# Banded attention and a PReLU feed-forward block in fp32: eight single PSUM banks in place of two double ones, x of a single tile taken bank by bank, and another table for the opening

## The chip, the cores and the metric

The kernel runs on one core of a Trainium2 chip. The metric is the time of one execution on the device in microseconds (us), the median of three executions. TensorE (PE) multiplies and writes to PSUM, which has eight banks of 128 x 512 fp32 numbers. VectorE (DVE), ScalarE (ACT) and GpSimd (POOL) work on SBUF, the first two on PSUM as well, and SyncE (SP) issues most of the DMAs. Each engine takes its instructions in the order in which the program lists them, so one that waits holds up all behind it on its engine.

## The reference

```python
def _attn_ref(q, k, v) -> np.ndarray:        # 8 batches, 8 heads, 576 positions, 64 wide
    B, H, S, D = q.shape
    window = 64
    scale = 1.0 / np.sqrt(D)
    scores = scale * np.matmul(q, k.transpose(0, 1, 3, 2))
    pos = np.arange(S)
    rel = pos[:, None] - pos[None, :]
    mask = (rel >= 0) & (rel < window)
    scores = np.where(mask, scores, -1000000000.0)
    scores = scores - np.max(scores, axis=-1, keepdims=True)
    attn = np.exp(scores)
    attn = attn / (np.sum(attn, axis=-1, keepdims=True) + 1e-09)
    return np.matmul(attn, v).astype(np.float32)

def _moe_ref(x, w_in, w_out, alpha) -> np.ndarray:   # x 4608 x 512, w_in 512 x 2048, w_out 2048 x 512
    h = x @ w_in
    g = np.maximum(h, 0.0) + alpha * np.minimum(h, 0.0)
    return (g @ w_out).astype(np.float32)
```

The output of the attention, with the heads side by side, is x of the second function.

## The kernel before

**Tiles and stages.** The 4608 rows are 36 tiles of 128. Four tiles make a block n of 512 rows, so there are nine blocks. The first stage does the attention of a tile t and the first product of each block; the second stage (from about 500 us) does the second product with seven products of halves in place of eight (`second(n)`). Every fp32 product is made of three passes over a high and a low part: for the first product xh with wh, xl with wh, and xh with wl.

**Attention of a tile** runs over the engines in this order. The names are those of the planner and of the texts: `s` the scores (PE, `score`, L447), `le` the mask and the row's maximum of one head (DVE, `take_least`, L456, eight for a tile), `ex` the exponential (ACT, L463, eight), `rc` the reciprocal of the sums (DVE, L467 and L468), `sc` the scaling (POOL, L472, two halves u of a tile), `tu` the turning by PE (L487, one for each half), `td` the copy of what was turned out of PSUM (ACT, L491, one for each half), `av` the product with v (PE, L503), `xh` the copy of the high part of x (ACT, L575) and `xl` the low part (DVE, L577). Tiles 0 to 7 go through alone (`attend_one`), with one pair of banks for all of it: banks 2 and 3 for even tiles, 4 and 5 for odd ones (`S_BANK`). Half u is turned into bank u of the pair. The tiles after that go two at a time (`attend_two`).

**Weights.** w_in is loaded in 16 chunks f, as 64-bit words that hold doubles. `chunk` makes floats of one: `rd` (ACT, L352), `rb` (DVE, L356, or ACT, L359), `sh` (DVE, L367), `sg` (DVE, L369) and `jn` (POOL, L371); `split` then makes its high part `wi.f.h` (ACT or POOL, L325) and its low part `wi.f.l` (POOL, L322). `REBIASED` lists the chunks whose `rb` goes to DVE.

**Cells.** `cell(n, f)` is the product of block n with chunk f, `h.n.f` (L644), into bank 0 or 1 by turns; ACT and DVE then take it out of the bank (`sl` L650, `la` L651). Of block 0 the first three cells are done as halves: `h.0.f.0` with tiles 0 and 1, `h.0.f.1` with tiles 2 and 3.

**The small table.** `signs` is four DVE instructions on 128 x 16 numbers in SBUF (L312 to L315). `ident` is a constant matrix; PE multiplies it with itself (`warm`, L307) wherever the plan finds nothing else for PE before `h.0.1.0`.

**Order.** `Program.order` plays the work through with a duration for each operation and writes each engine's order out. `SINGLE` gives the begin of each single tile, `HALVES` that of the half cells; `key=` and `earliest=` set what comes first. The tile framework then puts a wait in front of an instruction for each buffer that it shares with earlier ones. Banks 2 and 3 are one PSUM buffer of 1024 columns (`twins[0]`), and banks 4 and 5 another (`twins[1]`); the others have a buffer each. In the built program a matmul into one bank of a twin waits for a reader of the other bank, and a reader of one bank for the matmuls into the other that stand ahead of it.

**Second stage.** A block n has seven sums, in the order 1, 2, 6, 7, 5, 3, 4, in seven of the eight banks; the next block begins at the bank that follows. `O.u.i` (L748) is the product i of step u, with u = 4n to 4n + 3. At the end of a block, `u1` (ACT, L765) and `d11`, `u2`, `u3`, `u4`, `d22`, `d12`, `d21` (DVE, L756) add the sums up, each reading one bank, and four DMAs store the results (L762).

Of the kernel before, what the change touches and what calls it, by code (L numbers as in the profile page):

```python
# [9 lines left out]
F32 = mybir.dt.float32  # L10
# [14 lines left out]
CELL = 3.25  # L25
UNIT = 9.55
STEP = 1.362
SINGLE = (3.0, 3.0, 11.0, 15.0, 21.0, 32.0, 35.0, 41.0)
HALVES = (14.0, 19.0)
EARLY_HALVES = 3  # L30
PACE = 3.6
FIRST_TURN = 60.0
REBIASED = (0, 1, 2, 3, 4, 5, 6, 7, 8, 9, 10, 11, 12, 13, 14, 15)
PE_TURNED = (9, 17, 25, 33)
CONVERT_AT = {1: 0, 3: 1, 5: 2, 7: 3}
LAGS = {"PE": 0.25, "DVE": 0.14, "ACT": 0.13, "POOL": 0.10, "SP": 0.0}
# [157 lines left out]
def banded_attention_then_prelu_ffn(  # L194
# [11 lines left out]
    nc = tc.nc  # L206
    P = 128
# [20 lines left out]
    psum = ctx.enter_context(tc.tile_pool(name="psum", bufs=1, space=PSUM))  # L228
# [4 lines left out]
    xs = [[const.tile([P, NP, BT * P], F32R, name=f"x{x}_0") for x in "hl"]]  # L233
# [28 lines left out]
    staged = [stage[:, i] for i in range(2)]  # L262
    raws.append(stage.rearrange("p x t -> p (x t)").bitcast(I32))

    banks = [psum.tile([P, 512], F32, name=f"bank_{i}") for i in range(2)]
    twins = [psum.tile([P, 1024], F32, name=f"bank_{2 + 2 * i}") for i in range(2)]
    banks += [twin[:, x * 512:(x + 1) * 512] for twin in twins for x in range(2)]
    banks += [psum.tile([P, 512], F32, name=f"bank_{i}") for i in (6, 7)]
    H_BANK, S_BANK, V_BANK = (0, 1), ((2, 3), (4, 5)), (6, 7)

    hidden = [[far.tile([P, 4, 2, HW], F32, name=f"g_{n}_{d}") for d in range(DUOS)] for n in range(NB)]
# [2 lines left out]
    def halves_of(*bs):  # L274
        return [f"bank.{b}.{i}" for b in bs for i in range(2)]

    p = Program()

    def add(name, engine, busy, emit, *args, **kw):
        p.add(name, {engine: (busy, emit)}, *args, **kw)  # L280
# [54 lines left out]
    def chunk(name, c, f, second, start=0.0):  # L335
# [17 lines left out]
        aside, k_aside = banks[V_BANK[c % 2]], halves_of(V_BANK[c % 2])  # L353
        by_vector = not second and f in REBIASED
        if by_vector:
# [80 lines left out]
    def bank_of(i):  # L436
        return banks[i].rearrange("p (e k) -> p e k", e=NP)
# [123 lines left out]
    def x_keys(part, slot, tiles=range(BT)):  # L561
        return [f"{part}.{slot}.{i}" for i in tiles]

    def x_parts(ts, by=V_BANK):
        n, i = divmod(ts[0], BT)
        here = slice(i * P, (i + len(ts)) * P)
        if len(ts) == 1:
            pieces = [(range(2), [part.rearrange("p (a x) t -> p x a t", x=2)[:, :, :, here] for part in xs[n % 2]],
                       twins[ts[0] % 2].rearrange("p (x i a q) -> p x i a q", x=2, i=2, a=2)[:, :, 0], halves_of(*by))]
        else:  # L570
            pieces = [([x], [part.rearrange("p (a x) (i q) -> p x i a q", x=2, q=P)[:, x, i:i + 2] for part in xs[n % 2]],
                       bank_of(V_BANK[x]).rearrange("p (i a) q -> p i a q", i=2), halves_of(V_BANK[x])) for x in range(2)]
        for x, to, from_, k in pieces:
            his, los = ([key for a in range(2) for y in x for key in x_keys(part, 4 * (n % 2) + 2 * a + y, range(i, i + len(ts)))] for part in ("xh", "xl"))
            p.add(f"xh.{ts[0]}.{x[0]}", {"ACT": (0.48, lambda to=to, from_=from_: nc.scalar.copy(to[0], from_)),  # L575
                                         "DVE": (0.6, lambda to=to, from_=from_: nc.vector.tensor_copy(to[0], from_))}, k, his)
            add(f"xl.{ts[0]}.{x[0]}", "DVE", 0.61, lambda to=to, from_=from_: nc.vector.tensor_tensor(  # L577
                out=to[1], in0=from_, in1=to[0].bitcast(F32), op=ALU.subtract), [*k, *his], los)

    def attend_one(t, begin, pace):  # L580
# [10 lines left out]
    def values_of(ts, key):  # L591
        def emit():
            for i, t in enumerate(ts):
                value(t, i)

        add(f"av.{ts[0]}", "PE", 2.0, emit, [*(k for t in ts for k in ring_keys("v", t)), *(k for t in ts for k in pt_keys(t))], halves_of(*V_BANK), key=key)
        x_parts(ts)
# [25 lines left out]
    def begin_of(n):  # L623
        return BEGIN + n * CELL * NF
# [155 lines left out]
    add("masks", "POOL", 3.2, guard_and_masks, (), ["masks", "sums"])  # L780
    for t, begin in enumerate(SINGLE):
        attend_one(t, begin, 5.0)
    for f in range(NF):
        convert_in(f)
    pair = lambda j: [t for t in (2 * j, 2 * j + 1) if t < NT]
    attend_two(pair(len(SINGLE) // 2), FIRST_TURN, [])
    for n in range(NB):
        for j, f in ((2 * n + 3, 4), (2 * n + 4, 12)):
            if j > len(SINGLE) // 2 and pair(j - 1):
                attend_two(pair(j), begin_of(n) + (f - 0.5) * CELL, pair(j - 1))  # L790
# [3 lines left out]
        if n == 0:  # L794
            for f in range(EARLY_HALVES):
                cell(n, f, HALVES[0] + f * PACE, 0)
            whole = NF - EARLY_HALVES
            for f in range(max(EARLY_HALVES, whole)):
                if f < EARLY_HALVES:
                    cell(n, f, HALVES[1] + f * PACE, 1)  # L800
                if f < whole:
                    cell(n, EARLY_HALVES + f, HALVES[1] + (f + 0.5) * PACE)
        if n in CONVERT_AT:
# [56 lines left out]
```

## Time and profile before

| | us |
|---|---|
| median of three runs | 857.07 |
| lowest and highest | 854.37, 858.63 |
| the profiled execution: time | 860.36 |
| the profiled execution: span on the core | 858.6 |
| PE busy (share of the span) | 847.6 (99%) |
| DVE busy | 696.8 (81%) |
| ACT busy | 438.2 (51%) |
| POOL busy | 201.9 (24%) |

The span runs from the first to the last event on the core; the execution's own time is 1.8 us longer. PE is busy nearly throughout, so the time is PE's work, what PE waits, what it loses to a lower clock or spends on `warm`, and what comes behind its last matmul.

### The profile page before, as it was taken

The page shows a single profiled execution, that of the slowest core. Times are in us where ns is not written, and L with a number is a line of the kernel's source. Part 1 is how long each engine was busy: PE and PEld are TensorE (multiplying, and loading weights), DVE is VectorE, ACT ScalarE, POOL GpSimd, SP SyncE. Part 2 cuts the span into 40 slices and gives each one's busy share as a digit, 9 for nine tenths or more (in the row PEclk, how much of TensorE's full clock was granted, in tenths as well). Part 3 has the DMA queues.
Part 4 walks back from the last instruction along what each step waited for, and adds up shares of the span by engine and source line. Part 5 has one row for each costly group of instructions (what it writes and reads, how often), then busy time and mean ns, then how long its engine had stood idle before and what let it go on. Part 6 is the DMA issues. An engine that isn't in the chain of part 4 may idle for free.

```text
span 858.6 us, 21067 instructions
## 1 busy us (share of the span) xinstructions
PE 847.6 (99%) x7850; PEld 769.2 (90%) x7850; DVE 696.8 (81%) x1777; ACT 438.2 (51%) x1110; POOL 201.9 (24%) x190
## 2 busy tenths in 40 slices
PE   8899999999999999999999999999999999999997
PEld 8788888888888888888888899999999999999997
DVE  5797898998989989899876367978888786979783
ACT  6787765466454664457534244444444444444440
POOL 5788391116411363113720000000000000000000
PEclk9899999999999999999999999999999999999999
DMA  8787655565556666566447995544444343535201
GB/s 254 237 261 240 216 166 167 166 199 175 193 173 186 230 203 234 170 222 234 167 173 257 291 341 177 160 134 125 124 144 146 116 147 111 159 107 165 72 30 50
DMA packets 121287, 152.91 MB, mean 178 GB/s; under 512 B 10592, under 2 KB 92512, under 8 KB 121184
## 3 DMA queue, kind: packets, MB, share of 16 engines
q1 hardware_dynamic: 120896, 151.30, 55.2%
q8 instruction: 62, 1.02, 0.5%
q14 instruction: 41, 0.34, 0.1%
q10 hardware_dynamic: 288, 0.26, 0.1%
HBM read 95.95 MB, written 55.57 MB: 176 GB/s over the span
## 4 chain that ended last, share of the span: by engine, by line
PE 97%; ACT 1%; DVE 1%; issue 0%; POOL 0%; DVEq 0%; POOLq 0%
PE bank L644 46%; PE bank L748 41%; PE bank L503 4%; PE bank L447 4%; PE bank L487 1%; ACT w L463 1%; PE bank L307 1%; ACT pt L491 0%; DVE cell L756 0%; DVE xl L577 0%; DVE alphas L312 0%; ACT ulps L352 0%; DVE val L369 0%; POOL w L472 0%; DVE w L456 0%
## 5 line engine op out<-in xcount | busy, mean ns | idle before, releaser
L720 ACT CAST yh<-g 128x512 fp32r<-128x512 f32 x216 | 132.7, 621 | 146.2 <-PE bank L748 94.7
L650 ACT ACTIVATE cell<-bank,alphas 128x512 f32<-128x512 f32 (+1 forms) x147 | 99.8, 679 | 175.7 <-PE bank L644 168.9
L721 DVE TENSOR_TENSOR yl<-g,yh 128x512 fp32r<-128x512 f32 x216 | 147.7, 687 | 28.8 <-ACT yh L720 27.2
L748 PE MATMUL bank<-wh,yh 128*128 128x256 f32 x1008 | 159.0, 280 | 0.8 <-DVE cell L756 0.8
L748 PE MATMUL bank<-wh,yl 128*128 128x256 f32 x1008 | 158.9, 280 | 0.0
L748 PE MATMUL bank<-wl,yh 128*128 128x256 f32 x1008 | 158.9, 280 | 0.0
L644 PE MATMUL bank<-xh,wh 128*128 128x512 f32 (+1 forms) x588 | 158.6, 392 | 0.0
L644 PE MATMUL bank<-xl,wh 128*128 128x512 f32 (+1 forms) x588 | 155.3, 386 | 0.0
L644 PE MATMUL bank<-xh,wl 128*128 128x512 f32 (+1 forms) x588 | 154.6, 385 | 0.0
L651 DVE SCALAR_TENSOR_TENSOR cell<-bank,alphas,cell 128x512 f32<-128x512 f32 (+1 forms) x147 | 108.4, 739 | 55.5 <-ACT cell L650 51.0
L748 PEld LDWEIGHTS bank<-wh,yh 128*128 128x128 f32 x1008 | 136.5, 189 | 1.1 <-ACT yh L720 1.0
L748 PEld LDWEIGHTS bank<-wh,yl 128*128 128x128 f32 x1008 | 135.7, 189 | 0.0
L748 PEld LDWEIGHTS bank<-wl,yh 128*128 128x128 f32 x1008 | 135.6, 189 | 0.0
L644 PEld LDWEIGHTS bank<-xl,wh 128*128 128x128 f32 x588 | 109.6, 189 | 22.6
L644 PEld LDWEIGHTS bank<-xh,wl 128*128 128x128 f32 x588 | 109.3, 188 | 22.1
L644 PEld LDWEIGHTS bank<-xh,wh 128*128 128x128 f32 x588 | 107.6, 189 | 22.8 <-issue 0.5
L463 ACT ACTIVATE w<-w,nm 128x128 f32<-128x128 f32 x288 | 111.6, 391 | 23.2 <-DVE nm L456 23.2
L472 POOL TENSOR_TENSOR w<-w,rc 128x512 f32<-128x512 f32 x72 | 74.3, 1052 | 136.3 <-DVE rc L468 100.0
L480 DVE STREAM_TRANSPOSE pt<-w 32x256 f32<-32x256 f32 x192 | 83.7, 436 | 9.6 <-POOL w L472 6.1
L715 DVE TENSOR_TENSOR g<-g,g 128x512 f32<-128x512 f32 x108 | 74.2, 687 | 1.8
L456 DVE CUSTOM_DVE_ANT_0 w<-bank,masks 128x128 f32<-128x128 f32 x288 | 63.0, 286 | 8.7 <-PE bank L447 8.7
L482 DVE STREAM_TRANSPOSE pt<-w 32x128 f32<-32x128 f32 x192 | 58.1, 303 | 3.9
(62 smaller groups left out, 701.7 us busy)
## 6 DMA issues: line engine op xcount, KB each, us to landing
g<-g SPq DMA_DIRECT2D x144, 256.0 KB, 3.3
g<-cell SPq DMA_DIRECT2D x141, 256.0 KB, 3.1
out<-cell SPq DMA_DIRECT2D x36, 256.0 KB, 2.5
q<-qT SPq DMA_DIRECT2D x35, 256.0 KB, 5.0
raw<-w_out SPq DMA_DIRECT2D x16, 512.0 KB, 5.8
v<-vN SPq DMA_DIRECT2D x18, 384.0 KB, 5.1
k<-kT SPq DMA_DIRECT2D x17, 384.0 KB, 4.5
raw<-w_in SPq DMA_DIRECT2D x11, 512.0 KB, 5.4
```

The source lines that it names most:

```text
L456: nc.vector.tensor_tensor_reduce(out=of_head(weights[t % 2], g), in0=bank_of(S_BANK[t % 2][x])[:, e].rearrange("p (b k) -> p b k", b=2), i ...
L463: nc.scalar.activation(w, w, AF.Exp, scale=-1.0, bias=least[t % 2][:, g:g + 1], accum_out=sums[:, t % 2, g, 0:1])
L472: nc.gpsimd.tensor_tensor(out=w, in0=w, in1=rc.unsqueeze(1).unsqueeze(3).broadcast_to(list(w.shape)), op=ALU.mult)
L480: nc.vector.transpose(to, w[:, x, j])
L482: nc.vector.transpose(to[:, :, j ^ 1], w[:, x, j, :, j ^ 1])
L644: nc.tensor.matmul(h, w[KEPT + f][:, a * P:(a + 1) * P], v[:, a, half], start=k == a == 0, stop=k == 2 and a == NP - 1, skip_group_check=True)
L650: add(f"sl.{name}", "ACT", 0.13 + 0.46 * part, lambda: nc.scalar.activation(g, h, AF.Copy, scale=slope[:, f:f + 1]), ["signs", *k_h], k_g)
L651: add(f"la.{name}", "DVE", 0.12 + 0.61 * part, lambda: nc.vector.scalar_tensor_tensor(out=g, in0=h, scalar=sign[:, f:f + 1], in1=g, op0=AL ...
L715: add(name, "DVE", 0.61, lambda: nc.vector.tensor_tensor(out=to(), in0=a(), in1=b(), op=op), reads, writes)
L720: add(f"ys.{u}.{i}.h", "ACT", 0.54, lambda: nc.scalar.copy(y_of(y_hi, x, hi), value()), [*ks, "late"], his)
L721: add(f"ys.{u}.{i}.l", "DVE", 0.61, lambda: nc.vector.tensor_tensor(out=y_of(y_lo, x, lo), in0=value(), in1=y_of(y_hi, x, hi).bitcast(F32) ...
L748: nc.tensor.matmul(banks[bank][:, h * EH:(h + 1) * EH], part[:, j * HW + h * P:j * HW + (h + 1) * P], w[k][:, j * EH:(j + 1) * EH], start= ...
```

## The change

Each PSUM bank becomes a buffer of its own. For a single tile, x is copied (`xh`) and subtracted (`xl`) in two instructions of 256 columns, one for each bank, where one instruction of 512 columns took both. The chunks whose `rb` goes to DVE are six and no longer sixteen; the other ten go to ACT. Four numbers of the table of turns are others, and the planner's durations for the x of a single tile are those of the smaller pieces.

```diff
-SINGLE = (3.0, 3.0, 11.0, 15.0, 21.0, 32.0, 35.0, 41.0)
-HALVES = (14.0, 19.0)
+SINGLE = (3.0, 3.0, 11.0, 13.0, 23.0, 32.0, 37.0, 41.0)
+HALVES = (12.0, 19.0)
...
-REBIASED = (0, 1, 2, 3, 4, 5, 6, 7, 8, 9, 10, 11, 12, 13, 14, 15)
+REBIASED = (1, 4, 5, 7, 8, 9)
...
-    banks = [psum.tile([P, 512], F32, name=f"bank_{i}") for i in range(2)]
-    twins = [psum.tile([P, 1024], F32, name=f"bank_{2 + 2 * i}") for i in range(2)]
-    banks += [twin[:, x * 512:(x + 1) * 512] for twin in twins for x in range(2)]
-    banks += [psum.tile([P, 512], F32, name=f"bank_{i}") for i in (6, 7)]
+    banks = [psum.tile([P, 512], F32, name=f"bank_{i}") for i in range(8)]
...
-        here = slice(i * P, (i + len(ts)) * P)
-        if len(ts) == 1:
-            pieces = [(range(2), [part.rearrange("p (a x) t -> p x a t", x=2)[:, :, :, here] for part in xs[n % 2]],
-                       twins[ts[0] % 2].rearrange("p (x i a q) -> p x i a q", x=2, i=2, a=2)[:, :, 0], halves_of(*by))]
-        else:
-            pieces = [([x], [part.rearrange("p (a x) (i q) -> p x i a q", x=2, q=P)[:, x, i:i + 2] for part in xs[n % 2]],
-                       bank_of(V_BANK[x]).rearrange("p (i a) q -> p i a q", i=2), halves_of(V_BANK[x])) for x in range(2)]
+        copy, other, pass_ = (0.48, 0.6, 0.61) if len(ts) == 2 else (0.36, 0.34, 0.35)
+        pieces = [([x], [part.rearrange("p (a x) (i q) -> p x i a q", x=2, q=P)[:, x, i:i + len(ts)] for part in xs[n % 2]],
+                   bank_of(by[x]).rearrange("p (i a) q -> p i a q", i=2)[:, :len(ts)], halves_of(by[x])) for x in range(2)]
```

The order of the instructions differs in the opening alone (to `h.0.15` on PE); the first instructions to differ stand behind the exponentials of tile 1. Behind the opening the order is as before, and the bank buffers and the waits differ. Where rows of the two programs are set side by side, the lines of the changed kernel have smaller numbers (L367 of before is L364).

The first place is DVE between the second reciprocal of tile 1 and the first `le` of tile 2. `bank_6` and `bank_7` are where `sh` puts its result, `alphas` is the table of `signs`, `bank_2` (with `bank_3`) and `bank_4` (with `bank_5`) hold tiles 0 and 1. Before:

```order
L367 TENSOR_SCALAR bank_7_166<-bank_7_166 128x512
L577 TENSOR_TENSOR xl_0_120<-bank_2_163,xh_0_119 128x2x2x128
L369 SCALAR_TENSOR_TENSOR val_156<-raw_1_155,bank_7_166 128x512
L356 TENSOR_SCALAR bank_6_165<-stage_160 128x512
L312 TENSOR_SCALAR alphas_130<-alphas_130 128x16
L313 TENSOR_SCALAR alphas_130<-alphas_130 128x16
L314 TENSOR_TENSOR alphas_130<-alphas_130 128x16
L315 TENSOR_SCALAR alphas_130<-alphas_130 128x16
L577 TENSOR_TENSOR xl_0_120<-bank_4_164,xh_0_119 128x2x2x128
L367 TENSOR_SCALAR bank_6_165<-bank_6_165 128x512
L369 SCALAR_TENSOR_TENSOR val_156<-stage_160,bank_6_165 128x512
L456 ISA w_0_146,nm_0_150<-bank_2_163,masks_140 128x2x64
```

And now, in the same place (`xl` is L570, `signs` L309 to L312, `sh` L364, `sg` L366, `le` L453):

```order
L364 TENSOR_SCALAR bank_7_168<-bank_7_168 128x512
L366 SCALAR_TENSOR_TENSOR val_156<-raw_1_155,bank_7_168 128x512
L570 TENSOR_TENSOR xl_0_120<-bank_2_163,xh_0_119 128x2x128
L309 TENSOR_SCALAR alphas_130<-alphas_130 128x16
L310 TENSOR_SCALAR alphas_130<-alphas_130 128x16
L311 TENSOR_TENSOR alphas_130<-alphas_130 128x16
L312 TENSOR_SCALAR alphas_130<-alphas_130 128x16
L570 TENSOR_TENSOR xl_0_120<-bank_3_164,xh_0_119 128x2x128
L364 TENSOR_SCALAR bank_6_167<-val_156 128x512
L570 TENSOR_TENSOR xl_0_120<-bank_4_165,xh_0_119 128x2x128
L570 TENSOR_TENSOR xl_0_120<-bank_5_166,xh_0_119 128x2x128
L366 SCALAR_TENSOR_TENSOR val_156<-stage_160,bank_6_167 128x512
```

The low part of tile 0 stood whole ahead of `signs`; now its second half, out of bank 3, stands behind them, and the scores of tile 2, which go into banks 2 and 3, wait for both halves. `rb` of chunk 2 (L356) has gone to ACT.

The second place is POOL in the same stretch. `val` with `ulps` is `jn`, `wh_12` and `wl_12` are the parts of chunk 0, `wl_13` the low part of chunk 1. Before:

```order
L371 TENSOR_TENSOR val_156<-val_156,ulps_0_157 128x512
L325 CAST wh_12_75<-val_156 128x512
L322 TENSOR_TENSOR wl_12_103<-val_156,wh_12_75 128x512
L371 TENSOR_TENSOR val_156<-val_156,ulps_1_158 128x512
L322 TENSOR_TENSOR wl_13_104<-val_156,wh_13_76 128x512
```

And now:

```order
L368 TENSOR_TENSOR val_156<-val_156,ulps_0_157 128x512
L322 CAST wh_12_75<-val_156 128x512
L368 TENSOR_TENSOR val_156<-val_156,ulps_1_158 128x512
L319 TENSOR_TENSOR wl_12_103<-val_156,wh_12_75 128x512
L319 TENSOR_TENSOR wl_13_104<-val_156,wh_13_76 128x512
```

`jn` of chunk 1 now comes ahead of the low part of chunk 0; `wl_13` waits for `wh_13`, which ACT makes out of that `jn`.

The third place is the end of DVE's list, the adding up of the last block, `d11`, `u2`, `u3`, `u4`, `d22`, `d12`, `d21`. Before:

```order
L756 TENSOR_TENSOR cell_0_125<-bank_1_162,r_0_122 128x512
L756 TENSOR_TENSOR r_1_123<-bank_2_163,r_0_122 128x512
L756 TENSOR_TENSOR r_2_124<-bank_2_163,r_1_123 128x512
L756 TENSOR_TENSOR r_0_122<-bank_4_164,r_1_123 128x512
L756 TENSOR_TENSOR cell_3_128<-bank_4_164,r_2_124 128x512
L756 TENSOR_TENSOR cell_1_126<-bank_4_164,r_0_122 128x512
L756 TENSOR_TENSOR cell_2_127<-bank_6_165,r_2_124 128x512
```

And now:

```order
L749 TENSOR_TENSOR cell_0_125<-bank_1_162,r_0_122 128x512
L749 TENSOR_TENSOR r_1_123<-bank_2_163,r_0_122 128x512
L749 TENSOR_TENSOR r_2_124<-bank_3_164,r_1_123 128x512
L749 TENSOR_TENSOR r_0_122<-bank_4_165,r_1_123 128x512
L749 TENSOR_TENSOR cell_3_128<-bank_4_165,r_2_124 128x512
L749 TENSOR_TENSOR cell_1_126<-bank_5_166,r_0_122 128x512
L749 TENSOR_TENSOR cell_2_127<-bank_6_167,r_2_124 128x512
```

Nothing moved; the names of the buffers did. In the built program `u4` (the fourth row) waited for the matmuls of product 3, the last into the twin of banks 4 and 5; now it waits for those of product 5, the last into bank 4.

## Rows read from the trace of the kernel before

**Rows 1.** The profile's page: ACT's busy tenths in 40 slices; the last-ending chain by engine.
```profile
ACT  6787765466454664457534244444444444444440
...
PE 97%; ACT 1%; DVE 1%; issue 0%; POOL 0%; DVEq 0%; POOLq 0%
```

**Rows 2.** Chain that ended last, in order: start us, us, what.
```profile
23.30 6.27 ACT w L463 x32
...
31.82 1.99 PE bank L503 x48
...
37.84 1.06 PE bank L503 x48
```

**Rows 3.** Windows of 1 us: us, each engine's busy time, PE's granted clock, DMA.
```profile
30.00:31.00 1.00, 0.79 (x4) 0.56 (x4) 0.96 (x5) 0.63 (x2) 0.45 (x1) 0.69 0.14 50
...
37.00:38.00 1.00, 1.00 (x14) 0.86 (x17) 0.00 (x0) 1.00 (x3) 0.59 (x1) 0.90 0.05 17
```

**Rows 4.** Timeline of DVE: start us, us, instruction, idle before and releaser.
```profile
14.22 0.67 DVE L367 TENSOR_SCALAR bank<-bank 128x512 int32<-128x512 int32 x1
...
19.36 1.28 DVE L312 TENSOR_SCALAR alphas<-alphas 128x16 f32<-128x16 f32 x1
20.67 0.17 DVE L313 TENSOR_SCALAR alphas<-alphas 128x16 f32<-128x16 f32 x1
...
22.97 0.28 DVE L456 CUSTOM_DVE_ANT_0 w<-bank,masks 128x128 f32<-128x128 f32 x1
```

**Rows 5.** Timeline of POOL.
```profile
17.39 0.61 POOL L325 CAST wh<-val 128x512 fp32r<-128x512 f32 x1
18.09 1.29 POOL L322 TENSOR_TENSOR wl<-val,wh 128x512 fp32r<-128x512 f32 x1
19.33 1.27 POOL L371 TENSOR_TENSOR val<-val,ulps 128x512 int32<-128x512 int32 x1
21.33 1.27 POOL L322 TENSOR_TENSOR wl<-val,wh 128x512 fp32r<-128x512 f32 x1 [0.73 <-ACT wh L325]
```

**Rows 6.** Timeline at 85 us: a POOL and a DVE instruction.
```profile
84.80 1.30 POOL L322 TENSOR_TENSOR wl<-val,wh 128x512 fp32r<-128x512 f32 x1
...
85.29 1.09 DVE L361 TENSOR_SCALAR val<-val,alphas 128x512 int32<-128x512 int32 x1
```

**Rows 7.** Timeline of PE behind tile 1 and at the turning of tile 2.
```profile
19.92 1.83 PE L307 MATMUL bank<-ident 128*128 128x128 f32 x14
21.67 1.10 PE L447 MATMUL bank<-k,q 64*64 64x128 f32 x32
...
30.21 0.94 PE L487 MATMUL bank<-ident,w 128*128 128x128 f32 x4 [0.77 <-ACT pt L491]
```

**Rows 8.** Groups by line and form: costs of 256 columns (xcount, busy us, mean ns).
```profile
L651 DVE SCALAR_TENSOR_TENSOR cell<-bank,alphas,cell 128x256 f32<-128x256 f32 x6 | 2.8, 472 | 2.5 <-ACT cell L650 2.5
```

**Rows 9.** Timeline of ACT at the end of tile 3's exponentials.
```profile
29.10 0.39 ACT L463 ACTIVATE w<-w,nm 128x128 f32<-128x128 f32 x1
...
29.48 0.58 ACT L491 COPY pt<-bank 128x512 f32<-128x512 f32 x1
29.96 0.67 ACT L352 ACTIVATE ulps<-raw 128x512 int32<-128x512 uint32 x1
```

**Rows 10.** Timeline of DVE and PE in the second stage, at the third block.
```profile
584.47 0.68 DVE L756 TENSOR_TENSOR cell<-bank,r 128x512 f32<-128x512 f32 x1
...
585.29 0.71 PE L748 MATMUL bank<-wh,yh 128*128 128x256 f32 x4 [0.81 <-DVE cell L756]
```

**Rows 11.** Timeline of the end: DVE's last rows, PE's last, SP's last.
```profile
852.69 0.69 DVE L756 TENSOR_TENSOR r<-bank,r 128x512 f32<-128x512 f32 x1 [1.41 <-PE bank L748]
...
853.30 1.88 DVE L756 TENSOR_TENSOR cell<-bank,r 128x512 f32<-128x512 f32 x3
...
853.43 0.63 PE L748 MATMUL bank<-wh,yl 128*128 128x256 f32 x4
854.00 1.57 SPq L762 DMA_DIRECT2D out<-cell  x3
```

More of the change, by code (lines that the diff above doesn't have):

```diff
@@ L565, in x_parts @@
         n, i = divmod(ts[0], BT)
-        here = slice(i * P, (i + len(ts)) * P)
-        if len(ts) == 1:
-            pieces = [(range(2), [part.rearrange("p (a x) t -> p x a t", x=2)[:, :, :, here] for part in xs[n % 2]],
-                       twins[ts[0] % 2].rearrange("p (x i a q) -> p x i a q", x=2, i=2, a=2)[:, :, 0], halves_of(*by))]
-        else:
-            pieces = [([x], [part.rearrange("p (a x) (i q) -> p x i a q", x=2, q=P)[:, x, i:i + 2] for part in xs[n % 2]],
-                       bank_of(V_BANK[x]).rearrange("p (i a) q -> p i a q", i=2), halves_of(V_BANK[x])) for x in range(2)]
+        copy, other, pass_ = (0.48, 0.6, 0.61) if len(ts) == 2 else (0.36, 0.34, 0.35)
+        pieces = [([x], [part.rearrange("p (a x) (i q) -> p x i a q", x=2, q=P)[:, x, i:i + len(ts)] for part in xs[n % 2]],
+                   bank_of(by[x]).rearrange("p (i a) q -> p i a q", i=2)[:, :len(ts)], halves_of(by[x])) for x in range(2)]
         for x, to, from_, k in pieces:
             his, los = ([key for a in range(2) for y in x for key in x_keys(part, 4 * (n % 2) + 2 * a + y, range(i, i + len(ts)))] for part in ("xh", "xl"))
-            p.add(f"xh.{ts[0]}.{x[0]}", {"ACT": (0.48, lambda to=to, from_=from_: nc.scalar.copy(to[0], from_)),
-                                         "DVE": (0.6, lambda to=to, from_=from_: nc.vector.tensor_copy(to[0], from_))}, k, his)
-            add(f"xl.{ts[0]}.{x[0]}", "DVE", 0.61, lambda to=to, from_=from_: nc.vector.tensor_tensor(
+            p.add(f"xh.{ts[0]}.{x[0]}", {"ACT": (copy, lambda to=to, from_=from_: nc.scalar.copy(to[0], from_)),
+                                         "DVE": (other, lambda to=to, from_=from_: nc.vector.tensor_copy(to[0], from_))}, k, his)
+            add(f"xl.{ts[0]}.{x[0]}", "DVE", pass_, lambda to=to, from_=from_: nc.vector.tensor_tensor(
                 out=to[1], in0=from_, in1=to[0].bitcast(F32), op=ALU.subtract), [*k, *his], los)
```

## The prediction

> **What bounds the kernel now.** I read the profile from the whole to the stretch. The page first: the chain that ended last is PE for 97% of the span [rows 1], so an edit elsewhere counts only where PE waits for it. Then the chain in order of time: from 31.82 us, where `av` of tile 2 begins, it is PE work without a break to the end of the first stage, and in the second stage PE waits once. So the time is settled in three places: by when `av` of tile 2 can begin, by that one wait, and by what comes behind PE's last matmul.
>
> Up to 31.82 us the chain runs through other engines. PE has done tile 1 by 19.92 us, passes 1.83 us with `warm`, and starts the scores of tile 2 at 21.67 [rows 7]. DVE begins `le` of tile 2 at 22.97 [rows 4]. ACT then works 6.27 us at the exponentials of tiles 2 and 3 [rows 2], the last from 29.10 [rows 9]; only then come the copies `td` and `av`. PE's clock is the second thing to see: the granted clock falls within 30 to 31 us and is back within 37 to 38 [rows 3]; between lies half clock, 1.2 GHz in place of 2.4, behind a stretch in which PE mostly waited. `av` took 1.99 us there and 1.06 later [rows 2].
>
> The sum is made against the profiled execution, 860.36 us, which is 1.8 us above its span and 3.3 above the median of the three runs, 857.07. I carry the difference over to the median.
>
> **Step 1, the start of tile 2 (a wait is added).** The scores of tile 2 go into banks 2 and 3, so they wait for `xl` of tile 0 out of both. That was one instruction ahead of `signs`; now its second half stands behind `signs`. What `signs` cost is in the rows: its first instruction, on 16 columns, took 1.28 us, where the next took 0.17 [rows 4]. It began at 19.36 and ended at 20.64; POOL's `jn` ran from 19.33 to 20.60 [rows 5]. At 85 us the same: a DVE instruction from SBUF to SBUF, begun at 85.29, ended 0.28 behind the end of POOL's `wl` at 86.10 [rows 6]. So such a DVE instruction waits until POOL's is done. The other three of `signs` ran fast because POOL then stood idle 0.73 us, until 21.33, for `wh` from ACT [rows 5].
>
> When does this come now? Up to the exponentials of tile 1 nothing moved. `rb` of chunk 0 is behind them on ACT, 0.67 us by the row of another ACT instruction of that size [rows 9], so DVE begins `sh` at about 14.5 where it was 14.22 [rows 4]. Then come `sh`, `rb`, `sg`, `sh`, `sg`, five of about 0.65 us: 17.7. The first half of `xl` brings it to 18.0, and there `signs` begin. POOL can start `jn` of chunk 0 when the first `sg` is done, three instructions in, at 16.5. Its next five, by [rows 5], are 1.27, 0.61, 1.27, 1.29 and 1.27: 5.7 us, to 22.2. The idle time is gone, since `jn` of chunk 1 now comes 1.29 us earlier in POOL's list, and ACT has made `wh_13` (ready about 20.8) before POOL asks for it at 20.9. So the four instructions of `signs` meet a POOL that is never idle from 16.5 to 22.2.
>
> The bounds: if all four get through behind one POOL instruction, `signs` end at 18.8; if they wait for POOL's next idle time, at 22.6. I take 22.4, near the upper end, because of what happened at 19.36: DVE asked while POOL's `wl` (18.09 plus 1.29, so 19.38) still ran, and POOL's next, begun at 19.33, went first [rows 4, 5]; instructions that follow each other on POOL left no gap. Behind `signs` DVE has the second half of `xl`, `sh`, two halves of `xl` for tile 1, and `sg`. A half costs at most 0.47 [rows 8] and follows the one ahead about 0.33 later: 0.33 + 0.60 + 0.66 + 0.61 = 2.2 us. So `le` of tile 2 begins at 24.6, 1.6 later than 22.97. The scores of tile 2 are done by then (22.9 plus 1.1 [rows 7]); what is queued behind them on PE is the first half cell and the scores of tile 3, and ACT's exponentials wait for `le`. At the lower end PE sets it: fewer `warm` (10 matmuls for 14), so scores to about 21.9 and `le` at 22.0, which is 1.0 earlier than before.
>
> The Trainium skill ("SBUF — State Buffer", section "SBUF: two separate sides") says that DVE and GpSimd share a pair of ports as an exclusive lock that is held for the whole instruction, and that it binds DVE in a two-port mode or with two SBUF inputs. The trace agrees with 1.28 us for 16 columns, but shows a single instruction held up; by the rule each of the four must win the pair by itself, which gives the upper end (+1.6 us for `le`), while one hold-up as in the row would give the lower (-1.0).
>
> **Step 2, the turning of tile 2 (a wait is removed).** The second `tu` of tile 2 waited for ACT's copy of the first, 0.77 us, as both halves lay in one buffer [rows 7]. From the end of the last exponential, 29.4, to `av` at 31.82 it took 2.4 us. Now both `tu` are done before the exponentials end, and ACT goes on with a copy, `rb` of chunk 3 and a copy: 0.48 (the distance of the two starts) + 0.58 + 0.58 [rows 9], with 0.1 to reach PE 1.75. That is 0.65 earlier. `av` of tile 2 thus begins 1.6 - 0.65 = 1.0 us later than before, at 32.8; with the lower bound of step 1, 1.65 earlier. What stood late in its place is `ex` of tile 3, not `tu`.
>
> **Step 3, the rest of the opening (moved work).** ACT gets ten `rb` of 0.67 and a second `xh` for eight tiles; a pair of halves costs at most 2 x 0.47 - 0.67 = 0.27 more than a whole [rows 4, 8]. That is 8.9 us; in the first four slices of 21.5 us ACT was busy 6, 7, 8 and 7 tenths, so 26 us were idle [rows 1]. DVE loses ten `rb` and gains eight times 0.27: 4.5 us less. PE has cells of block 0 to cover both. I cost it at nothing; if the cover fails at one cell, PE waits for that cell's evacuation, below 1 us for each. The turns of tiles 4 to 7 stand among the cells, where PE waited for nothing.
>
> **Step 4, the second stage (a wait is removed).** PE's wait of 0.81 us at 585.29 is for DVE's `cell` begun at 584.47 [rows 10]. By the program that is `d21`, the reader of bank 5, while the matmul writes bank 4; now it waits for `d12`, which stands ahead of `d21` in DVE's list. I take -0.8, between 0 (if the low part it needs were as late) and -0.8.
>
> **Step 5, the end (a wait is removed).** `u4` read bank 4 at 852.69, behind the matmuls into bank 5, and three further sums followed from 853.30 for 1.88 us, to 855.18 [rows 11]. Now `u4` and `d22` run a product earlier, and `d21` starts with the end of PE's last matmul (853.43 + 0.63), so it ends at about 854.8: 0.4 sooner. The three stores that were issued together from 854.00 are spread, and the last moves 256 KB alone. Between -0.4 and -1.0; I take -0.7.
>
> **Sum:** +1.0 - 0.8 - 0.7 = -0.5 us: 859.9 against the profiled execution, 856.6 on the median.
>
> **The rivals.**
> *`signs` get through* (step 1 at its lower end): `av` of tile 2 1.65 earlier, so -1.65 - 0.8 - 0.7 = -3.2, 853.9 us. For it: 16 columns take 0.17 us. Against it: POOL's unbroken list.
> *The clock stays up behind tile 2.* PE's wait there becomes shorter, as both `tu` come sooner and `av` follows `ex` more closely. In before, PE work from 31.82 to about 37.1 ran at half clock, 5.3 us for what takes 2.65; without it 2.6 us are won: 854.0. Against it: PE still waits over 2 of the 4 us before `av`. With both rivals together 851.3.
> *The clock falls at the new wait* (slower): PE stands from about 20.5 to 22.9 for `xl`. If the granted clock falls there, the half cell (1.6 us) and the scores of tile 3 (1.1) take 2.7 us more. The exponentials of tile 3 then start late instead of right behind tile 2's; it decides once those scores end later than tile 2's exponentials. Some 2.4 us: 859.0.
>
> **How the numbers follow.** My forecast has 0.45, `signs` through 0.2, the clock up 0.15, both 0.05, the clock down 0.15. A measurement of this kernel tells about 0.5%, 4.3 us (its three runs lie that far apart): under 852.8 is faster, over 861.4 slower. Only both rivals together reach 852.8; with some of the two single ones, 1 to 2 us off, faster is 0.13. Slower takes the early clock plus cover that fails in step 3: 0.05. The range holds the cases from 853.9 to 859.0 with a microsecond for the runs' spread, 852.8 to 860.2. The likeliest alone: 855.2 to 858.
>
> **What the profile of the changed kernel would show.** Step 1: `signs` lasting from 18 to 22 us, several of the four longer than 1 us, `le` of tile 2 at 24 to 25. It is wrong if `le` comes before 22.97. Step 2: no wait of `tu` for `td`, `av` of tile 2 at about 32.8. Step 3: PE without a break from there. Step 4: no wait at 585. Step 5: `u4` 1.4 us earlier against PE's end, the last store alone. The whole is wrong if PE waits among the cells of block 0, or if the clock at 20 to 40 us differs.

## The result and the profile after

The changed kernel took 845.79 us (median of 4 executions, 844.68 to 848.35), the kernel before 857.2 beside it (854.37 to 858.63): ratio 0.9875, 95% interval 0.9839 to 0.9911. It is faster by 1.25%, and the prediction's range ended at 852.8. The profiled execution took 848.35 us with a span of 846.6; before it was 860.36 and 858.6. So 12.0 us are to be found in the trace.

The chain of the changed kernel, in order (start us, us, what; line numbers are 3 to 7 lower than before, L741 is the matmul of the second stage):

```profile
88.08 16.59 PE bank L637 x72
...
444.31 19.27 PE bank L637 x84
...
463.58 3.03 PE bank L637 x12
...
499.60 343.20 PE bank L741 x3024
```

The same places in the chain of before, whose opening is in [rows 2]:

```profile
88.85 16.59 PE bank L644 x72
...
445.07 54.63 PE bank L644 x240
499.69 83.44 PE bank L748 x732
...
585.29 267.37 PE bank L748 x2268
```

The opening, all that stands ahead of the row of 72, ends 0.77 us earlier (88.08 for 88.85). But at 463.58 and 466.65 PE waits for DVE to empty a bank (its weight loads stand idle 0.43 and 0.46 us; the 12 matmuls between take 3.03 us for 2.73), and the second stage begins at the same time (499.60, 499.69). The gain lies behind that. Before, 732 matmuls took 83.44 us, 0.1140 each, and the 2268 behind the wait of 0.81 us [rows 10] took 267.37, 0.1179 each. Now there is no wait, and all 3024 take 0.1135. Windows show when the pace changes; first of before (us, PE busy with its matmuls, granted clock, DMA share, GB/s), then of the changed kernel:

```profile
500.00:510.00 10.00, 10.00 (x87) 1.00 1.05 393
515.00:580.00 65.00, 65.00 (x576) 1.00 0.53 157
...
670.00:840.00 170.00, 170.00 (x1445) 1.00 0.36 111
```

```profile
500.00:510.00 10.00, 10.00 (x87) 1.00 1.05 387
515.00:580.00 65.00, 65.00 (x576) 1.00 0.50 151
...
670.00:840.00 170.00, 170.00 (x1502) 1.00 0.35 108
```

PE is 100% busy in every row, at full granted clock, on the same instructions. Up to 580 us the counts agree: slow at first, then fast. Behind the wait before stays slow: 1445 matmuls in 170 us for 1502, 0.1176 us each for 0.1132. (A window also counts the matmuls that cross its edges, one to three here, so these are a little low: from start to start the traces have 0.1178 and 0.1133, the two numbers used from here on. For the same reason a slow stretch of 10 us shows 87; at 560 us, where the pace is fast, 10 us show 91.) PE's timeline of before on both sides of the wait (its first row behind is the one in [rows 10]) shows it in the starts of groups of four:

```profile
583.41 0.62 PE L748 MATMUL bank<-wl,yh 128*128 128x256 f32 x4
583.87 0.62 PE L748 MATMUL bank<-wh,yl 128*128 128x256 f32 x4
...
585.84 0.63 PE L748 MATMUL bank<-wl,yh 128*128 128x256 f32 x4
586.31 0.63 PE L748 MATMUL bank<-wh,yl 128*128 128x256 f32 x4
```

0.46 us from group to group ahead of it (4 x 170 : 1502 = 0.453 by the windows), 0.47 behind. The gap itself put PE back by 1.06 us (1.42 from 583.87 to 585.29 and 0.55 to 585.84, for 0.45 each). Of the 3024 matmuls 62 products of 12 stand ahead of it, so 2280 behind: 2280 x (0.1176 - 0.1132) = 10.0 us. With the gap's 1.06, 0.09 at the stage's start and 0.73 behind PE's end (below) that is 11.9 of the 12.0.

The end, of the changed kernel, answers to [rows 11]:

```profile
842.17 0.62 PE L741 MATMUL bank<-wh,yl 128*128 128x256 f32 x4
842.82 0.69 DVE L749 TENSOR_TENSOR cell<-bank,r 128x512 f32<-128x512 f32 x1 [0.67 <-PE bank L741]
```

Only `d21` is left behind PE. From PE's last end (842.79; before 853.43 + 0.63 = 854.06) to the end of the span it is 3.8 us, before 4.6.

The opening, DVE and POOL, answers to [rows 4, 5]:

```profile
18.11 0.55 DVE L309 TENSOR_SCALAR alphas<-alphas 128x16 f32<-128x16 f32 x1
18.69 1.21 DVE L310 TENSOR_SCALAR alphas<-alphas 128x16 f32<-128x16 f32 x1
19.94 1.20 DVE L311 TENSOR_TENSOR alphas<-alphas 128x16 f32<-128x16 f32 x1
21.06 0.16 DVE L312 TENSOR_SCALAR alphas<-alphas 128x16 int32<-128x16 int32 x1
...
23.32 0.28 DVE L453 CUSTOM_DVE_ANT_0 w<-bank,masks 128x128 f32<-128x128 f32 x1
```

```profile
18.02 0.61 POOL L322 CAST wh<-val 128x512 fp32r<-128x512 f32 x1
18.59 1.28 POOL L368 TENSOR_TENSOR val<-val,ulps 128x512 int32<-128x512 int32 x1
19.83 2.57 POOL L319 TENSOR_TENSOR wl<-val,wh 128x512 fp32r<-128x512 f32 x2
```

Three of the four `signs` end with a POOL instruction each; the last takes 0.16 us, where POOL goes from one `wl` to the next.

### The profile page after: what moved, and what is told of

Read it like the earlier page. It is cut to its first block, busy times and chain, and to the rows that moved or that the text cites. A ratio compares the mean times of both kernels' runs of the same rounds, so it can differ in the third digit from the quotient of the medians.

```text
span 846.6 us, 21125 instructions
## 1 busy us (share of the span) xinstructions
PE 838.7 (99%) x7856; PEld 760.3 (90%) x7856; DVE 690.4 (82%) x1775; ACT 446.5 (53%) x1130; POOL 201.0 (24%) x188
## 4 chain that ended last, share of the span: by engine, by line
PE 97%; ACT 2%; DVE 1%; issue 0%; POOL 0%; POOLq 0%; DVEq 0%
PE bank L637 47%; PE bank L741 41%; PE bank L500 4%; PE bank L444 4%; ACT w L460 1%; PE bank L484 1%; PE bank L304 0%; DVE xl L570 0%; DVE val L366 0%; DVE bank L364 0%; ACT val L356 0%; DVE alphas L310 0%; ACT pt L488 0%; DVE cell L749 0%; DVE bank L353 0%
## 5 line engine op out<-in xcount | busy, mean ns | idle before, releaser
L741 PE MATMUL bank<-wh,yh 128*128 128x256 f32 x1008 | 155.4, 276 | 0.0
L741 PE MATMUL bank<-wh,yl 128*128 128x256 f32 x1008 | 155.4, 276 | 0.0
L741 PE MATMUL bank<-wl,yh 128*128 128x256 f32 x1008 | 155.4, 276 | 0.0
L644 DVE SCALAR_TENSOR_TENSOR cell<-bank,alphas,cell 128x512 f32<-128x512 f32 (+1 forms) x147 | 108.5, 739 | 54.7 <-ACT cell L643 47.8
L741 PEld LDWEIGHTS bank<-wh,yh 128*128 128x128 f32 x1008 | 133.2, 188 | 0.1
L741 PEld LDWEIGHTS bank<-wl,yh 128*128 128x128 f32 x1008 | 133.1, 188 | 0.0
L741 PEld LDWEIGHTS bank<-wh,yl 128*128 128x128 f32 x1008 | 133.1, 188 | 0.0
L453 DVE CUSTOM_DVE_ANT_0 w<-bank,masks 128x128 f32<-128x128 f32 x288 | 62.9, 285 | 9.5 <-PE bank L444 9.5
```

What stands on the lines that cost most here:

```text
L453: nc.vector.tensor_tensor_reduce(out=of_head(weights[t % 2], g), in0=bank_of(S_BANK[t % 2][x])[:, e].rearrange("p (b k) -> p b k", b=2), i ...
L644: add(f"la.{name}", "DVE", 0.12 + 0.61 * part, lambda: nc.vector.scalar_tensor_tensor(out=g, in0=h, scalar=sign[:, f:f + 1], in1=g, op0=AL ...
L741: nc.tensor.matmul(banks[bank][:, h * EH:(h + 1) * EH], part[:, j * HW + h * P:j * HW + (h + 1) * P], w[k][:, j * EH:(j + 1) * EH], start= ...
```

## The experiments

**Theory.** A wait of PE in the second stage can leave it at a slower pace, 0.1178 us per matmul for 0.1133, which lasts. **Rivals:** the tables of the opening bring the gain; the wait costs its own length alone; the pairs of banks slow the stage in some other way.

**1. The banks alone, and the tables alone.** The first takes the changed kernel with the old tables, the second the old kernel with the new ones:

```diff
-SINGLE = (3.0, 3.0, 11.0, 13.0, 23.0, 32.0, 37.0, 41.0)
+SINGLE = (3.0, 3.0, 11.0, 15.0, 21.0, 32.0, 35.0, 41.0)
...
-REBIASED = (1, 4, 5, 7, 8, 9)
+REBIASED = (0, 1, 2, 3, 4, 5, 6, 7, 8, 9, 10, 11, 12, 13, 14, 15)
```

> The eight banks as eight buffers and the copies of x bank by bank, with the three tables of the kernel before. Pace theory: the trace of the changed kernel starts a matmul of the second stage every 0.1133 us to its end, that of before only until the wait at 583.26 and every 0.1178 us behind it; the wait hangs on the pair of banks 4 and 5 alone, so the banks alone bring nearly all of the gain: 845 to 848 us, 3024 matmuls of the second stage in about 343 us. Rival, the tables (another order of the opening and other turns in the first stage bring the pace): about 856, 0.8 us under before for the wait that is gone, with the pace of 0.1178 somewhere in the second stage.

> The three tables of the change in the kernel before, with its pairs of banks. Pace theory: the wait of the product that writes bank 4 for the total that reads bank 5 stays, the matmuls behind it start every 0.1178 us, and the time is that of before within 1.5 us (855.5 to 858.5). Rival, the tables: 846 to 848 us.

The banks alone: 846.53 us, ratio to before 0.9859 (0.9829 to 0.9889). The tables alone: 861.63, ratio 1.0037 (1.001 to 1.0064), 2 to 3 us slower than before and over the 1.5 us expected; its second stage runs as before's does, from a start 2 us later. Their chains, second stage (banks, then tables):

```profile
497.38 343.20 PE bank L741 x3024
```

```profile
587.36 267.37 PE bank L748 x2268
```

With pairs of banks wait and slow pace are there whatever the tables; without them neither. The tables as the cause fall. A second run of the banks alone, on another occasion:

> The eight single banks with the three tables of before once more, on one chip with the others. If the tables of the change are worth something with single banks, it lies over the changed kernel's 844.3 us (its own earlier runs: 846.5, on another chip, where before was 1.2 us slower); if not, 844 to 845.

847.29 us, ratio 0.9855 (0.9835 to 0.9875). The changed kernel, run twice more, has 0.9827 (0.9799 to 0.9856) and 0.9846 (0.9822 to 0.9871). So this run lies over 844.3 us, the sign named for a worth of the tables, but the changed kernel ran on other chips, and by the ratios the tables with single banks are worth between 2.7 us and less than nothing: not settled here. One thing shows only with both, the clock of the opening (part 5).

**2. One pair at a time.** In the changed kernel banks 4 and 5 in one buffer again; in the kernel of the banks alone, banks 2 and 3:

```diff
-    banks = [psum.tile([P, 512], F32, name=f"bank_{i}") for i in range(8)]
+    banks = [psum.tile([P, 512], F32, name=f"bank_{i}") for i in range(4)]
+    twin = psum.tile([P, 1024], F32, name="bank_4")
+    banks += [twin[:, x * 512:(x + 1) * 512] for x in range(2)]
+    banks += [psum.tile([P, 512], F32, name=f"bank_{i}") for i in (6, 7)]
```

> The changed kernel with banks 4 and 5 alone in one buffer again. Pace theory: the wait of about 0.8 us comes back at about 583 us, and behind it every matmul of the second stage starts 0.1178 us after the last instead of 0.1133: 2268 x 0.0044 = 10.1 us and the wait's 1 to 2 us, so 855 to 858 us. Rival, the wait costs its own length alone: 846.6 to 847.6 us.

> The changed kernel with banks 4 and 5 in one buffer, a second time: of its ten executions three took 846.4 to 849.2 us and seven 855.3 to 859.4, and the one with a trace is of the three; there VectorE ends the total that reads bank 5 early enough for a wait of 0.1 us, after which the pace is 0.1133 again within five matmuls. Pace theory: an execution of 855 to 859 us has a wait of about 0.8 us or more at 580 to 586 us and 0.1178 us per matmul behind it; one of 846 to 849 has a short wait or none and 0.1133. Rival: an execution over 855 us whose second stage runs at 0.1133 us to its end, with the time lost elsewhere.

> The kernel of the single banks with the tables of before, banks 2 and 3 alone in one buffer again (banks 4 and 5 apart). Pace theory: no wait at 583 us; at product 119 (660 us) bank 2 waits for the total that reads bank 3, some 0.1 us as in the trace of the run with one repetition, and the pace behind it is 0.1133 again soon (846 to 848 us) or 0.1178 for the 1596 matmuls that are left (7.1 us: 853 to 855), each in some of the executions; none as long as before's 857 to 861. Rival, the pair of banks 2 and 3 is what slows the stage from 585 us on: 856 to 860 us.

Banks 4 and 5: two groups of executions, seven at 855.3 to 859.4 us and three at 846.4 to 849.2; the repetition was a single execution of 846.02. Both traces are of the lower group. So an execution of the higher group was not seen in a trace: that its 9 us are the slow pace is argued from the time alone, and the second of these expectations stays untested. What the first trace shows is a wait too short for a row of its own:

```profile
582.91 0.62 PE L744 MATMUL bank<-wh,yl 128*128 128x256 f32 x4
583.47 0.71 PE L744 MATMUL bank<-wh,yh 128*128 128x256 f32 x4
584.02 0.62 PE L744 MATMUL bank<-wl,yh 128*128 128x256 f32 x4
584.47 0.62 PE L744 MATMUL bank<-wh,yl 128*128 128x256 f32 x4
```

PE comes 0.1 us late at 583.47 and is at 0.45 per four again at 584.02. Banks 2 and 3: nine executions at 855.2 to 856.5, one at 848.7. That is above the 853 to 855 expected, with the opening's clock down in all ten, and reaches the rival's 856; the trace decides between them. It is of the nine; PE's timeline, and a window on each side of it:

```profile
660.33 0.62 PE L744 MATMUL bank<-wh,yl 128*128 128x256 f32 x4
660.88 0.71 PE L744 MATMUL bank<-wh,yh 128*128 128x256 f32 x4
661.43 0.63 PE L744 MATMUL bank<-wl,yh 128*128 128x256 f32 x4
```

```profile
600.00:650.00 50.00, 50.00 (x443) 1.00 0.47 137
675.00:835.00 160.00, 160.00 (x1361) 1.00 0.37 112
```

No wait at 583 us, and fast pace up to 660 (443 in 50 us). There a wait of 0.1 us, as short as the one above, is followed by the slow pace to the end: 1361 matmuls in 160 us where the fast pace makes 1414. The odd execution lies 7 us lower, as 1596 matmuls x 0.0044 would have it. So the rival that the pairs slow the stage all along falls: this pair does it from its own wait on. And the length of a wait does not decide alone.

**3. What ends the slow pace.** The stage begins slow (87 in 10 us) and turns fast at about 511 us in both kernels. The kernel keeps its operands in ten buffers; a list gives the column at which each product's operands lie, in steps of 16, in buffers 4 to 7. Products 5 to 8 have four different places, all others one:

```diff
-    SHIFTS = [(1, 1)] * 4 + [(i, i) for i in range(4)] + [(1, 1)] * 280
+    SHIFTS = [(1, 1)] * 288
```

is the one run, in the changed kernel, and in the kernel before the four places come once or twice more:

```diff
-    SHIFTS = [(1, 1)] * 4 + [(i, i) for i in range(4)] + [(1, 1)] * 280
+    SHIFTS = [(1, 1)] * 4 + [(i, i) for i in range(4)] + [(1, 1)] * 56 + [(i, i) for i in range(4)] + [(1, 1)] * 220
```

> The changed kernel with every product of the second stage at place 16 of its operand buffer, products 5 to 8 too. Pace theory, with the four places as what ends the slow pace: the stage begins at 0.1178 us per matmul, as in every trace so far (97 matmuls of it in the changed kernel's), and nothing ends it: 2927 x 0.0044 = 13.0 us over the changed kernel, 857 to 861 us, with no wait of the stage anywhere. Rival, the loads of weights or the products' own waits end it: 844 to 848 us.

> The kernel before, whose operand buffers 4 to 7 hold products 5 to 8 of the second stage at places 0, 16, 32 and 48 columns from the buffer's start (all later ones at 16), with the same four places once more for the products 65 to 68, two products behind the wait. In the trace of before the pace goes from 0.1178 to 0.1133 us per matmul as products 5 to 8 end (511 us). Pace theory, with the places as what ends the slow pace: the wait at 583 stays with its 0.8 us, the slow pace lasts some 80 matmuls instead of 2268, and the time falls by 2190 x 0.0044 = 9.7 us to 846 to 849. Rival one, something else ended it at 511 (the loads of weights, which fill the DMA engines until about 520): the slow pace stays, 856 to 858. Rival two, the wait costs its own length alone and the pace has nothing to do with it: no difference from before.

> The kernel before with the four places after the wait at 583 us and once more for the products 125 to 128, behind product 119, at which the trace of the run with one repetition shows a second wait (0.1 us at about 660, bank 2 for a total that reads bank 3) and the slow pace from there on. Pace theory: both slow stretches last some 80 matmuls, and the pairs of banks cost their waits and 0.7 us of slow pace: 846 to 850 us. Rival, the pairs cost more than waits and pace: above 852 us.

Without the places: 857.81 us, ratio to before 0.9993 (0.9973 to 1.0013); nine executions at 857.1 to 861.4, and one of 1407.38 us at a mean granted clock of 0.557, which has no trace and is left out of the ratio. The whole gain is gone, though no wait is there. Its chain:

```profile
495.39 356.17 PE bank L741 x3024
``` 

356.17 for 343.20 us, 13.0 more, as worked out. With the places once more in the kernel before: 857.56 (0.9932 to 1.0016 of before), so by the time alone the theory had failed. Its trace says otherwise (PE's timeline as the repeated products end, then windows):

```profile
593.86 0.63 PE L748 MATMUL bank<-wh,yl 128*128 128x256 f32 x4
594.33 0.62 PE L748 MATMUL bank<-wh,yh 128*128 128x256 f32 x4
...
595.24 0.62 PE L748 MATMUL bank<-wh,yl 128*128 128x256 f32 x4
```

```profile
600.00:650.00 50.00, 50.00 (x444) 1.00 0.42 131
675.00:835.00 160.00, 160.00 (x1361) 1.00 0.36 113
```

The slow pace ends at 594 us, 9 us behind the wait: 0.47 from group to group, then 0.91 for two. At 662 us the other pair's wait brings it back. In the trace of before there is none: PE, slow, comes to that product at 664.5, and DVE's `cell` ended at 664.15. Three of the ten executions, at 850.3 to 851.4 for 857.3 to 859.1, are 7 us lower, as if it had not. With the places a third time, behind that second wait: 851.51 us (four executions, 851.1 to 851.7), ratio 0.9903 (0.988 to 0.9925), above the 846 to 850 expected by its late opening (88.95 us, clock fallen, as late as before's), not by the second stage:

```profile
585.40 258.02 PE bank L748 x2268
```

9.35 us less than the 267.37 of before, with both pairs and both waits in place. But in this trace the places had nothing to end. The wait at 585 us is as long as before's (0.82 us), and PE is back at the fast pace behind it ahead of the repeated places, which begin at 588.22. So it is behind the second wait ahead of the third set, which begins at 670.27. PE's timeline at both:

```profile
586.40 0.62 PE L748 MATMUL bank<-wh,yl 128*128 128x256 f32 x4
...
588.22 0.64 PE L748 MATMUL bank<-wh,yh 128*128 128x256 f32 x4
...
663.02 0.62 PE L748 MATMUL bank<-wh,yl 128*128 128x256 f32 x4
...
669.82 0.62 PE L748 MATMUL bank<-wh,yl 128*128 128x256 f32 x4
```

Four groups in 1.82 us and 15 in 6.80 are 0.455 and 0.453 each. Neither wait left a slow pace here, and why all four executions lie low stays open. That the places end the pace rests on the other runs: on its end at 511 us in both kernels, on the stage that has no such places and stays slow, and on the trace that turns fast at 594.

**4. A wait made by hand.** In the changed kernel, without any pair:

```diff
...
                                 done += 1
+                                if u == 24 and i == 4 and done == 8:
+                                    first = y_of(y_lo, x, lo)[:, 0:1]
+                                    nc.vector.tensor_copy(tick[0], banks[bank])
+                                    nc.vector.tensor_copy(first, first.bitcast(F32))
...
```

> The changed kernel with one wait put into its second stage, far from any pair of banks: in product 173 of 252 (the last of tile block 25 by its fourth quarter), behind 8 of its 12 matmuls, VectorE copies the bank to a buffer that nothing reads and then one column of the low operand onto itself, and the last 4 matmuls read that operand. PE waits for the two copies, some 1.0 us (a pass of 512 columns 0.68, the two ways between the engines). Pace theory: the matmuls behind it, 79 products of 12, start every 0.1178 us instead of 0.1133: 1.0 + 948 x 0.0044 = 5.2 us over the changed kernel, 849 to 851. Rival, a wait costs its own length alone: 845 to 846. Rival two, only a wait at the start of a block of tiles (a bank's first matmul) does it: 845 to 846 too, with a fast pace behind the wait.

Six executions from 845.5 to 850.5 us, median 846.37. The traced one took 850.5:

```profile
496.54 238.03 PE bank L742 x2096
...
735.40 109.58 PE bank L742 x928
```

0.1136 us per matmul ahead of the wait (0.84 us idle), 0.1181 behind it, to the end: near the theory's 0.1178. Four of the others, at 845.5 to 846.4, leave room for the wait and little else; the fifth, of 848.49, had a mean granted clock of 0.996 for their 1.0. So by the median the rivals would have it, but the trace shows that a wait can leave the slow pace behind it. It does not always: the last trace of part 3 has a wait of 0.82 us and no slow pace behind it, and of the kernel before's 60 executions beside these runs two, of 847.71 and 849.88 us, lie 10 us below most of the others (855.1 to 861.8), as they would without the slow pace. Neither of the two has a trace.

**5. The opening.** Two versions were to keep TensorE busy, and its clock up, in PE's gaps at 27 to 31 us with more filler matmuls (and the first of them begins the second stage with buffer 4). Both laid the fillers into bank 7, in which the conversion of `w_in` keeps a value: the weights that they compute with are not those of `w_in`, and the work is the same.

> The changed kernel with two additions: 23 more of the opening's filler matmuls (8 behind the first half cell of function block 1, 4 and 11 behind the two turns of tile 2), into bank 7, which the opening leaves alone; and the second stage begins with buffer 4, so that products 1 to 4 have the four places. Theory that the granted clock falls over PE's idle time at 27.5 to 31.5 us of the opening: it stays at 1.0, the half-rate stretch of 6.8 us goes, about 3 us less where the changed kernel has it, and with the pace fast from product 5 instead of 9 another 0.2 us: 842 to 843.5 us, little spread. Rival, the clock falls all the same, or what the opening gains is waited off at the loads at 455 to 466 us: 844.5 to 847.

> The changed kernel with the fillers of the run before at half their number (4, 2 and 5: each is two matmuls of 0.11 us in the trace, so that 23 of them took 5 us and put the opening back by 4), bank 7 for them, and the buffers of the second stage in their usual turn. Theory of the clock: PE has no gap over 0.3 us at 27 to 31 us, the granted clock stays at 1.0, and all executions lie near the lower ones of the changed kernel: 843 to 844.5 us, against 844.3 to 844.5 and now and then 847. Rival, the fillers delay the turns of tile 2 by what they save: 845 to 848.

850.26 and 848.04 us: the granted clock stays at 1.0 in both traces, but the fillers waited for DVE in that bank, and the first version's took 5 us of PE by themselves. The opening ended at 88.66 and 87.12 us. With columns that nothing else uses, 11 fillers and again buffer 4 first, and the changed kernel beside it (its third expectation below is of an earlier run, beside those of part 3):

```diff
-        nc.tensor.matmul(banks[H_BANK[1]][:, :P], ident, ident, start=True, stop=True)
+        nc.tensor.matmul(banks[H_BANK[1]][:, 2 * P:3 * P], ident, ident, start=True, stop=True)
...
+            for _ in range({"h.0.1.0": 4, "tu.2.0": 2, "tu.2.1": 5}.get(o.name, 0)):
+                warm()
```

> The changed kernel with the opening's fillers in columns 256 to 383 of bank 1, which the half cells leave free (in the two runs before they lay in bank 7, which the conversion of the weights uses: there they waited for VectorE, put the opening back, and left wrong weights, of the same work), 11 more of them (4 behind the first half cell of function block 1, 2 and 5 behind the turns of tile 2), and the second stage beginning with buffer 4, so that products 1 to 4 have the four places. Theory of the clock: no gap of PE at 27 to 31 us, granted clock 1.0, the opening's end at 84 to 85 us in every execution, and the fast pace from product 5: 843 to 844.5 us with little spread, 0 to 2 us under the changed kernel beside it. Rival, what is gained in the opening is waited off at the loads at 455 to 466 us: the same time as the changed kernel within 0.5 us.

> The changed kernel as it is, on the same chip: 844 to 847 us, its executions apart by up to 4 us as the clock of the opening falls or not.

> The changed kernel once more, beside the others: 844.5 to 848.5 us by its earlier times. It says what the version with the tables of before and single banks (846.5 us, on its chip) is to be compared with, and whether its second stage runs at 0.1133 us per matmul from about 511 us in another execution too.

846.07 us (845.12 to 846.47) with fillers; 844.85 (844.48 to 846.83) and 844.34 (843.93 to 847.42) without. The clock stayed up in all five executions (0.999 or 1.0), and the rival stands: no gain, but 1.2 us lost against the changed kernel beside it. The chains at the end of the first stage, with fillers and then of the changed kernel (the execution of 843.93 us):

```profile
441.70 11.12 PE bank L637 x48
...
455.82 7.11 DMA g<-g
...
497.95 342.94 PE bank L741 x3024
```

```profile
84.20 16.59 PE bank L637 x72
...
440.38 54.70 PE bank L637 x240
495.09 343.20 PE bank L741 x3024
```

The early places bring 0.26 us (342.94 for 343.20). But of the first stage's last 240 matmuls, 54.7 us when nothing waits, the version with fillers lost 1.5 to the loads of the second stage. The changed kernel's two further traces have no fall of the clock, although PE waits in them at the same four places of the opening and about as long; a window of the changed kernel's first trace, then the same of the one shown last (PE, PEld, DVE, ACT, POOL, granted clock, DMA share, GB/s):

```profile
31.00:32.00 1.00, 0.54 (x14) 0.54 (x17) 0.97 (x2) 1.00 (x3) 1.00 (x2) 0.50 0.07 26
```

```profile
31.00:32.00 1.00, 1.00 (x28) 0.88 (x21) 1.00 (x3) 1.00 (x3) 1.00 (x2) 1.00 0.00 0
```

The opening ends at 88.08 us with the half rate and at 84.20 without; 1.15 of these 3.9 us are there before the clock falls (`signs` begin at 18.11 and 16.96). The executions of the changed kernel differ accordingly: 844.7 us at a mean granted clock of 1.0, 846.85 at 0.997, 848.35 at 0.996. How often the clock stays up, a mean of 0.999 or 1.0, depends on the kernel: 8 of 12 executions of the changed one, 6 of 60 of before beside these runs, 1 of 8 with the banks alone, 1 of 10 with the tables alone. By these counts it takes both halves of the change. Of the versions tried none is faster than the changed kernel.

## Why the prediction was wrong

**Step 4 failed.** It put the wait at "-0.8, between 0 and -0.8", as if a wait cost its own length. The mechanism of its removal was right (no wait at 585 us), and the gap itself was worth 1.06 us; but the wait set PE's pace for the 2280 matmuls behind it: 10.0 us, for which the sum had no term. The trace of before had the numbers: its chain has 83.44 us for 732 matmuls ahead of the wait and 267.37 for 2268 behind it. The prediction read there where PE waits, and not how fast it runs when it doesn't; "the time is settled in three places" left out the fourth. No rival held it either. The terms that the sum had measured 1.9 us together (0.09, 1.06 and 0.73), so without the pace the result would have lain in its range. Parts 1 to 4 show the cause: the wait goes with the pair (1), the pair of banks 2 and 3 slows the stage from its own wait on (2), the pace can be ended with the wait in place (3), a wait without a pair can begin it (4). What they leave open is how often a wait does it.

**Step 1** had the mechanism and missed the size: `signs` were held up by POOL's unbroken list, but lasted from 18.11 to 21.2 us, not to 22.4, since they got one instruction through for each of POOL's. `le` of tile 2 came at 23.32: 0.35 late for 1.6. The bounds (-1.0 to +1.6) held it. As the prediction read the rule of the Trainium skill ("SBUF — State Buffer", section "SBUF: two separate sides"), all four had to win the ports; the trace shows it for three.

**Step 2** was right in kind: the second `tu` no longer waits for `td`, and `av` of tile 2 went on at 31.46, 0.36 earlier than before, for 1.0 later; the difference is that of step 1. **Step 3**, costed at nothing, held: PE's chain has no other break up to 463 us. There 0.68 of the 0.77 us gained in the opening went, on banks that DVE emptied late: it stood at work for the second stage, held up by ACT, which had waited for a load until 460.19. No step had this. **Step 5** is right: 0.73 us for 0.7.

Of the rivals, `signs` did not get through, and the clock did not fall at the new wait (1.00 from 18 to 30 us). The clock that stays up came in most executions of the changed kernel, 8 of 12 for 6 of 60 of before (part 5), and the prediction gave it 0.2 in all. Its ground held as well: PE worked 2.9 of the 5 us from 27 to 32, 1.8 before. In the profiled execution the clock fell, as in before's [rows 3], so the 12.0 us above hold nothing of it; the medians do, since the executions of the changed kernel in which it stays up are 2 to 4 us lower.

**Open:** why a wait leaves the slow pace in one trace and not in another (one of 0.8 us in four of five, one of 0.1 us in two of five), what in the operands' places ends it, and what lets the clock fall in some executions of one kernel and not in others.

## What to carry to other kernels

Where a long row of equal matmuls is cut by a wait, divide time by count on both sides of it: a wait may cost far more than its length, and then the price grows with what is left behind it. Two banks in one buffer make such waits between parts that have nothing to do with each other. And an edit that leaves the time the same may still have worked: the trace of part 3 showed the slow pace ended, and there again behind the next wait.

## What the hardware showed that was not expected

The same matmuls (128 x 128 weights, 256 columns) run at two paces at full granted clock: 1502 in 170 us and 1445 in 170, 0.1133 and 0.1178 us from start to start. The slow one is there from the stage's first matmul. Later it begins behind a gap of PE: in four of five traces with one of 0.8 us, and in two of five with one of 0.1 us. It held for all 3024 matmuls where nothing ended it (356.17 us), and ended in every trace in which it met four products whose operands lie at 0, 16, 32 and 48 columns. The Trainium skill ("TensorE: Matmul & The Clock Gate", section "Back-to-back issue gap") has one spacing for a size, 262 cycles at 256 columns for a single matmul, an estimate of 0.109 us at 2.4 GHz, and says that in a stream weight loads and matmuls set it together. The runs show two spacings for one stream, both above that.
